# Plain fp32 instead of split halves in the inverse transforms of the first block of an H3 + MLP kernel

## The chip, the cores and the metric

The kernel runs on one core of one Trainium2 chip. The time is device microseconds of one execution. Before the change three runs took 2944.61, 2939.34 and 2942.58 us, median 2942.58. One more execution was taken by the hardware profiler: it took 2937.48 us, and the span from its first to its last instruction is 2935.7 us. Engines are named as in the profile: PE (TensorE matmul), PEld (its weight loads), DVE (VectorE), ACT (ScalarE), POOL (GpSimd), SP (SyncE, which here issues every DMA).

## The reference

Two layers A (a gated long convolution) and B (a two-layer MLP with squared ReLU) are applied in turn, twice, with a layer norm ahead of each. All is fp32, S = 2048 tokens, D = 1024 channels, F = 3584.

```python
def _A_ref(q, k, v, shift_k, ssm_k, ssm_D):
    ...
    kv = k_shift * v                      # k_shift: causal conv of k, 4 taps
    L = 2 * S
    kv_f = rfft(kv padded to L);  kf_f = rfft(ssm_k padded to L)
    y = irfft(kv_f * kf_f)[:S]
    y = y + kv * ssm_D
    return q * y

def _B_ref(x, w1, b1, w2, b2):
    h = jnp.einsum("bsd,df->bsf", x, w1) + b1
    r = jnp.where(h > zero, h, zero)
    return jnp.einsum("bsf,fd->bsd", r * r, w2) + b2

x = A_q
x = x + _A_ref(_layernorm(x), A_k, A_v, A_shift_k, A_ssm_k, A_ssm_D)
x = x + _B_ref(_layernorm(x), B_w1, B_b1, B_w2, B_b2)
x = x + _A_ref(...)          # the same two layers again
x = x + _B_ref(...)
```

The convolution in A does not depend on x, so the kernel computes it once per token block and uses it in both layers.

## The kernel before

Tokens go in four blocks of 512, channels in eight groups of 128. The convolution of a block is computed through short transforms written as matmuls with 128x128 tables of cosines and sines: forward transforms of kv (`x_part`) and of the kernel `ssm_k` (`g_part`), products of the spectra, sums, and inverse transforms. To keep fp32 accuracy on TensorE, an operand is split into a high half (a copy into the type `F32R`, made by ACT) and a low half (the rest, a subtraction by DVE or POOL), and `mm3` (L269 to L272) multiplies hi by hi, hi by lo and lo by hi into the same PSUM bank.

The work falls into two parts. `first_block` (L816) computes the convolution of block 0 for all channels, the first layer's A for it, and the first matmuls of B; in the profile it fills about the first 206 us. After that a fixed loop over matmul steps runs the MLPs of all (layer, block) pairs, while the convolutions of blocks 1 to 3 (`fwd_x`, `fwd_g`, `prod_stream`) are fed in between, step by step. The order of instructions in that loop does not depend on what `first_block` does.

In `first_block` every operation is a task of a planner (`Plan`, L86 to L169): it has a list of engines that may run it with an assumed cost for each, the keys that it reads and writes, and the ring buffers that it uses. `run` goes through the tasks greedily by assumed start times, and so fixes which engine runs a task (V is DVE, A is ACT, G is POOL, D is a DMA issue on SP) and the order on each engine. A change of tasks or assumed costs therefore reorders the whole block. A ring with n buffers makes a task wait, in the plan and on the chip, for the users of the buffer n places back.

For each channel group c the block runs `x_part`, `g_part` and then `prods(c, jj)` (L1001) for the two halves jj = 0, 1 of the block: 16 calls of `prods` in all. One call does, in this order: three products of spectra (L1009 for jj = 0; L1013 and the addition L1015 for jj = 1) into `sm` (ring of 2), two combinations (L1019, L1020), the butterfly (L538, L539) that gives z[0] and z[1], 128x256 each, and then the part that the change touches:

- L1021 takes the buffers `yl` and `yh`, rings of one buffer each;
- L1027, ACT copies z[h] into its half of `yh`, for h = 0 and 1;
- L1028, DVE or POOL subtracts: `yl` = z[h] - `yh`, for h = 0 and 1;
- L1031 calls `inverse` on the slice of 128 columns that belongs to jj: four `mm3`, 12 matmuls of 128 columns, into a bank of the ring `pt` (two banks), with the split tables `ih`, `il`, `fh`, `fl`;
- L1037 (DVE, twice) multiplies the result with the normalized x, L1040 (ACT) copies it out for `YD`, L1045 (POOL or DVE, twice) adds it to `x1`.

`inverse` (L545) is also called by `prod_stream` (L487) for blocks 1 to 3, there on all 256 columns. After the last `prods` of a half, `tail` (L1048) normalizes `x1`, transposes it (L1061) and splits it for the first matmuls of B (`weight`, L1072). The loads at the start of the block are issued at L1098 to L1100: the first kernel rows, k and v, and the table `praw`.

Of the kernel before, what the change touches and what calls it, by code (L numbers as in the profile page):

```python
# [10 lines left out]
F32 = mybir.dt.float32  # L11
F32R = mybir.dt.float32r
# [7 lines left out]
P = 128  # L20
# [7 lines left out]
BL = 256  # L28
# [143 lines left out]
def v_cost(n):  # L172
    return 130 + 1.04 * n


def g_cost(n):
    return 130 + 2.25 * n


def a_cost(n):  # L180
    return 170 + 0.84 * n
# [3 lines left out]
def tile_h3_mlp(ctx: ExitStack, tc: tile.TileContext, q, kT, vT, shk, ssmT, ssmD, w1, b1, w2, b2,  # L185
                fwd_t, pro_t, inv_t, sgn_t, out):
    nc = tc.nc
    V, A, G, PE, SY = nc.vector, nc.scalar, nc.gpsimd, nc.tensor, nc.sync
    ENG = {"V": V, "G": G}
# [3 lines left out]
    cv = ctx.enter_context(tc.tile_pool(name="cv", bufs=1))  # L193
# [75 lines left out]
    def mm3(o, lh, ll, rh, rl, start, stop):  # L269
        PE.matmul(o, lh, rh, start=start, stop=False)  # L270
        PE.matmul(o, lh, rl, start=False, stop=False)  # L271
        PE.matmul(o, ll, rh, start=False, stop=stop)  # L272
# [263 lines left out]
    def butterfly(E, s):  # L536
        y = s[:, 1:3].rearrange("p r (j u c) -> p u (r j) c", u=2, c=CG)
        E.tensor_add(flat(s, 0), y[:, 0], y[:, 1])  # L538
        E.tensor_sub(y[:, 0], y[:, 0], y[:, 1])  # L539
        return [t.rearrange("p (r n) c -> p r n c", r=2) for t in (flat(s, 0), y[:, 0])]  # L540
# [1 line left out]
    def own(t, e, g):  # L542
        return t[:, e].rearrange("p r (j g c) -> p r j g c", j=BT, g=2)[:, :, :, g % 2]

    def inverse(o, yh, yl, n=slice(0, BL)):  # L545
        tabs = ((ih[:, 1], il[:, 1], ih[:, 0], il[:, 0]), (fh[:, 3], fl[:, 3], fh[:, 2], fl[:, 2]))
        w = n.stop - n.start
        for e, (sh, sl, ch, cl) in enumerate(tabs):
            oe = o[:, e * w:e * w + w]
            mm3(oe, sh, sl, yh[:, e, 0, n], yl[:, e, 0, n], True, False)  # L550
            mm3(oe, ch, cl, yh[:, e, 1, n], yl[:, e, 1, n], False, True)

    def stats(x, mv):
        st = pre.tile([P, 2, 6], F32, name="st", bufs=2)
# [261 lines left out]
    def first_block():  # L816
        b = ORDER[0][1]
        pl = Plan()

        def new(pool, tag, n, shape, dt=F32):  # L820
            return pl.buf(tag, n, lambda: pool.tile(shape, dt, name=tag, bufs=n))
# [3 lines left out]
        def sub(tag, n, off, shape, dt=F32):  # L825
            size = math.prod(shape[1:])
            i = len(pl.rings.get(tag, ())) % n

            def make():
                v = big[dt].t[:, off + i * size:off + i * size + size]  # L830
                return v if len(shape) == 2 else v.rearrange("p (a b) -> p a b", a=shape[1])
            return pl.buf(tag, n, make, big[dt])

        def bank(tag, n, fn):
            return pl.buf(tag, n, fn)

        def dma(dst, src, r=(), w=(), cost=740, key=None):
            pl.add([("D", cost)], lambda e: SY.dma_start(dst(), src()), r, w, lat=2000)

        with tc.tile_pool(name="pro", bufs=1) as pro:  # L840
# [19 lines left out]
            def kv_load(c):  # L860
                k4 = sub("k4", 3, 0, [P, T + 3])
                v4 = new(cv, "fx", 4, [P, T])
                dma(lambda: k4.t, lambda: kT[c * P:(c + 1) * P, 0:T + 3], w=[k4])
                dma(lambda: v4.t, lambda: vT[c * P:(c + 1) * P, 0:T], w=[v4])
                return k4, v4
# [135 lines left out]
            def prods(c, jj):  # L1001
                sm = new(cv, "sm", 2, [P, 3, 2, CU])
                xs, gs = spec["x", c], spec["g", c]
                n = BL * (jj + 1)
                for ty, (xi, gi) in enumerate(PAIRS):
                    xt, gt = xs[xi], gs[gi]
                    opts = [("G", g_cost(n)), ("V", v_cost(n) + VX)]
                    if jj == 0:
                        pl.add(opts, lambda e, ty=ty, xt=xt, gt=gt: ENG[e].tensor_mul(  # L1009
                            sm.t[:, ty], xt.t[:, :, 0], gt.t[:, :, 0]), [xt, gt], [(sm, ty)])  # L1010
                        continue
                    pr = new(pro, "ppr", 3, [P, 2, BT, CU])
                    pl.add(opts, lambda e, xt=xt, gt=gt, pr=pr: ENG[e].tensor_mul(  # L1013
                        pr.t, xt.t, gt.t[:, :, ::-1]), [xt, gt], [pr])
                    pl.add([("V", v_cost(BL)), ("G", g_cost(BL) + 300)], lambda e, ty=ty, pr=pr: ENG[e].tensor_add(  # L1015
                        sm.t[:, ty], pr.t[:, :, 0], pr.t[:, :, 1]), [pr], [(sm, ty)])
                two = [("G", g_cost(BL)), ("V", v_cost(BL) + VX)]
                fl_ = lambda: sm.t.rearrange("p k g c -> p k (g c)")
                pl.add(two, lambda e: ENG[e].tensor_add(fl_()[:, 1], fl_()[:, 0], fl_()[:, 1]), [(sm, 0)], [(sm, 1)])  # L1019
                pl.add(two, lambda e: ENG[e].tensor_sub(fl_()[:, 2], fl_()[:, 0], fl_()[:, 2]), [(sm, 0)], [(sm, 2)])  # L1020
                yl, yh = new(cv, "yl", 1, [P, 2, 2, BL], F32R), new(cv, "yh", 1, [P, 2, 2, BL], F32R)  # L1021
                z = {}
                mine = lambda t, h: t[:, h, :, jj * P:jj * P + P].rearrange("p r (g c) -> p r g c", g=2)
                pl.add([("V", 2 * v_cost(BL) + VX), ("G", 2 * g_cost(BL))], lambda e: z.update(
                    enumerate(butterfly(ENG[e], fl_()))), [], [(sm, 0), (sm, 1), (sm, 2)])
                for h in range(2):
                    pl.add([("A", a_cost(BL))], lambda e, h=h: A.copy(mine(yh.t, h), z[h]), [(sm, h)], [(yh, h)])  # L1027
                    pl.add([("V", v_cost(BL)), ("G", g_cost(BL))], lambda e, h=h: ENG[e].tensor_sub(  # L1028
                        mine(yl.t, h), z[h], mine(yh.t, h).bitcast(F32)), [(sm, h), (yh, h)], [(yl, h)])
                o = bank("pt", 2, pst)  # L1030
                pl.add([("PE", 820)], lambda e: inverse(o.t, yh.t, yl.t, slice(jj * P, jj * P + P)), [(yh, 0), (yh, 1), (yl, 0), (yl, 1)], [o])  # L1031
                yo = new(cv, "fx", 4, [P, BL]) if c == KT - 1 else sub("praw", 1, 2840, [P, BL])
                yn = new(cv, "fk", 2, [P, 2, P])
                sl = slice(c * P, (c + 1) * P)
                for e_ in range(2):
                    tt = 2 * jj + e_
                    pl.add([("V", v_cost(P))], lambda e, e_=e_, tt=tt: V.scalar_tensor_tensor(  # L1037
                        yn.t[:, e_], o.t[:, e_ * P:e_ * P + P], 1.0 / BL, ns[tt].t[:, sl],
                        op0=OP.mult, op1=OP.mult), [o, (ns[tt], c // 4)], [(yn, e_)])
                pl.add([("A", a_cost(256))], lambda e: A.activation(  # L1040
                    yo.t, o.t[:, 0:BL], AF.Copy, scale=1.0 / BL), [o], [yo])
                dma(lambda: YD[0][:, 2 * jj:2 * jj + 2, sl], lambda: yo.t.rearrange("p (e c) -> p e c", e=2), [yo], cost=400)
                for e_ in range(2):
                    tt = 2 * jj + e_
                    pl.add([("G", g_cost(P)), ("V", v_cost(P) + VX)], lambda e, e_=e_, tt=tt: ENG[e].tensor_add(  # L1045
                        x1[tt].t[:, sl], x1[tt].t[:, sl], yn.t[:, e_]), [(yn, e_)], [(x1[tt], c)])
# [51 lines left out]
            gl = g_load(0)  # L1098
            kv = kv_load(0)
            dma(lambda: praw.t, lambda: pro_t, w=[praw], cost=1460)  # L1100
            pl.add([("A", a_cost(1024))], lambda e: A.copy(ptab.t[:, 0:8], praw.t), [praw], [ptab])
            pl.add([("V", v_cost(1024))], lambda e: V.tensor_sub(
                ptab.t[:, 8:16], praw.t, ptab.t[:, 0:8].bitcast(F32)), [praw], [ptab])
            for c in range(KT):
                x_part(c, *kv)
                g_part(c, *gl)
                if c + 1 < KT:
                    gl = g_load(c + 1)
                    kv = kv_load(c + 1)
                if c == 0:  # L1110
                    for t in range(NT):
                        ln_part(t)
                for jj in range(BT):
                    prods(c, jj)
                    if c == KT - 1:
                        tail(2 * jj)
                        tail(2 * jj + 1)
# [4 lines left out]
        n = 2 * AHEAD_0  # L1122
# [5 lines left out]
        return [x.t for x in xT]  # L1128

    xT = first_block()  # L1130
    pds = prod_stream()
    ml = ctx.enter_context(tc.tile_pool(name="ml", bufs=1, reuse_waits="tile"))
# [151 lines left out]
    for sb in range(1, NB):  # L1284
        if WIN[sb] > lo_u:
# [3 lines left out]
            n = sum(last_step[u] + 1 - start_step[u] - 19 * (1 - PREP_PACE) for u in range(lo_u, hi_u))  # L1289
# [16 lines left out]
    for s, (k, u, c, a, i, tts, w) in enumerate(steps):  # L1306
# [17 lines left out]
        if k == "m1":  # L1324
# [19 lines left out]
            o = rs[c, a]["o"]  # L1344
            for kk in range(4):
                t = slice(kk * P, (kk + 1) * P)
# [5 lines left out]
        else:  # L1352
            if i == 0:
                os = {tt: ps2() for tt in tts}
            r = rs[c, i]
            for tt in tts:
                t = slice(tt * P, (tt + 1) * P)
# [21 lines left out]
        if u + 1 < NU and not direct[u]:  # L1379
            n = s - start_step[u]  # L1380
# [80 lines left out]
```

## Time and profile before

| stretch of the span (us) | what runs | PE busy | DVE busy | ACT busy | POOL busy | granted PE clock |
|---|---|---|---|---|---|---|
| 0 to 206 | first block | 153.15 | 160.48 | 67.12 | 111.51 | 0.78 |
| 206 to 500 | matmul loop, convolutions beside it | 256.39 | 208.52 | 117.49 | 131.47 | 0.93 |
| 500 to 1000 | the same | 464.86 | 376.04 | 182.28 | 215.43 | 0.97 |
| 1000 to 2000 | the same | 990.24 | 682.94 | 345.67 | 425.53 | 1.00 |
| 2000 to 2935 | matmul loop | 929.47 | 279.69 | 265.69 | 33.31 | 1.00 |

The profiled execution took 2937.48 us with a span of 2935.7 us; the median of the three runs is 2942.58 us. The table is read by stretch: from 1000 us on PE is busy nearly all the time at full clock, while in the first block no engine is. "Granted PE clock" is the share of the full TensorE clock that the throttle let through, averaged over the stretch. Matmuls are pipelined in the records, each is shown until its modelled end, so the distance from one start to the next (here called the pitch) tells what a matmul costs in a row of them, and not its duration.

### The profile page before, as it was taken

The page shows a single profiled execution, that of the slowest core. Times are in us where ns is not written, and L with a number is a line of the kernel's source. Part 1 is how long each engine was busy: PE and PEld are TensorE (multiplying, and loading weights), DVE is VectorE, ACT ScalarE, POOL GpSimd, SP SyncE. Part 2 cuts the span into 40 slices and gives each one's busy share as a digit, 9 for nine tenths or more (in the row PEclk, how much of TensorE's full clock was granted, in tenths as well). Part 3 has the DMA queues.
Part 4 walks back from the last instruction along what each step waited for, and adds up shares of the span by engine and source line. Part 5 has one row for each costly group of instructions (what it writes and reads, how often), then busy time and mean ns, then how long its engine had stood idle before and what let it go on. Part 6 is the DMA issues. An engine that isn't in the chain of part 4 may idle for free.

```text
span 2935.7 us, 36250 instructions
## 1 busy us (share of the span) xinstructions
PE 2794.1 (95%) x13104; PEld 2328.6 (79%) x13104; DVE 1707.7 (58%) x2583; ACT 978.2 (33%) x1721; POOL 917.3 (31%) x649
## 2 busy tenths in 40 slices
PE   6878889879999999999999999999999999999999
PEld 6776767668888888878888888888888888888887
DVE  7867677776877777787875774353223522252122
ACT  3234434424233423444222422343223422242222
POOL 5634365433644264433655275201000100001000
PEclk8779999989999999999999999999999999999999
DMA  6357898777988889878887778565545755475543
GB/s 205 124 177 247 290 339 282 245 284 245 335 292 298 311 287 329 271 270 322 301 311 255 282 281 316 171 222 212 203 162 175 252 197 171 159 262 162 182 143 127
DMA packets 321572, 711.76 MB, mean 242 GB/s; under 512 B 31208, under 2 KB 123504, under 8 KB 321392
## 3 DMA queue, kind: packets, MB, share of 16 engines
q1 hardware_dynamic: 321392, 709.44, 70.3%
q8 instruction: 103, 1.69, 0.2%
q14 instruction: 77, 0.63, 0.1%
HBM read 578.24 MB, written 131.07 MB: 242 GB/s over the span
## 4 chain that ended last, share of the span: by engine, by line
PE 77%; DVE 10%; DMA 7%; issue 2%; POOL 2%; ACT 1%; SPq 1%; DVEq 0%; POOLq 0%; ACTq 0%
PE p L271 24%; PE p L270 24%; PE p L272 24%; DMA cg<-gd 3%; DVE whl L778 1%; PE pt L271 1%; PE pt L272 1%; POOL cp L443 1%; PE pt L270 1%; DMA xd<-fx 1%; DVE sm L447 1%; DMA wd_m<-whl 1%; PE p L649 1%; DMA whl<-wd_m 1%; DVE fx L300 1%
## 5 line engine op out<-in xcount | busy, mean ns | idle before, releaser
L443 POOL TENSOR_TENSOR cp<-cx,cg 128x384 f32<-128x384 f32 (+5 forms) x288 | 527.7, 1848 | 749.3 <-DMA cg<-gd 587.4
L271 PE MATMUL p<-whl,rh 128*128 128x512 f32 x1792 | 713.4, 398 | 15.8 <-DVE whl L778 14.1
L270 PE MATMUL p<-whl,rh 128*128 128x512 f32 x1792 | 716.0, 400 | 2.0 <-DMA whl<-wd_m 1.9
L270 PE MATMUL p<-xh,whl 128*128 128x512 f32 (+1 forms) x1840 | 708.7, 385 | 6.0 <-ACT wr L1141 4.0
L272 PE MATMUL p<-xh,whl 128*128 128x512 f32 (+1 forms) x1840 | 706.7, 384 | 5.8 <-DVE whl L778 5.8
L272 PE MATMUL p<-whl,rl 128*128 128x512 f32 x1792 | 711.9, 397 | 0.0
L271 PE MATMUL p<-xl,whl 128*128 128x512 f32 (+1 forms) x1840 | 706.5, 384 | 0.0
L1149 DVE TENSOR_TENSOR rl<-wr,rh 128x512 fp32r<-128x512 f32 x224 | 196.5, 877 | 545.0 <-ACT rh L1144 544.8
L778 DVE TENSOR_TENSOR whl<-wr,whl 128x512 fp32r<-128x512 f32 x403 | 360.9, 900 | 171.1 <-ACT whl L770 169.5
L271 PEld LDWEIGHTS p<-whl,rh 128*128 128x128 f32 x1792 | 341.2, 190 | 96.3 <-DVE whl L778 17.7
L770 ACT CAST whl<-wr 128x512 fp32r<-128x512 f32 x410 | 251.7, 618 | 469.5 <-PE p L272 363.5
L272 PEld LDWEIGHTS p<-xh,whl 128*128 128x128 f32 x1840 | 348.5, 189 | 74.5 <-DVE whl L778 6.2
L270 PEld LDWEIGHTS p<-xh,whl 128*128 128x128 f32 x1840 | 349.3, 190 | 72.8 <-ACT wr L1141 4.2
L270 PEld LDWEIGHTS p<-whl,rh 128*128 128x128 f32 x1792 | 341.1, 190 | 80.1 <-DMA whl<-wd_m 2.3
L272 PEld LDWEIGHTS p<-whl,rl 128*128 128x128 f32 x1792 | 340.7, 190 | 80.0
L271 PEld LDWEIGHTS p<-xl,whl 128*128 128x128 f32 x1840 | 349.0, 190 | 65.8 <-DVE xl L1068 0.3
L1141 ACT ACTIVATE wr<-p,b1t 128x512 f32<-128x512 f32 x222 | 153.2, 690 | 699.4 <-PE p L272 693.2
L1269 POOL TENSOR_TENSOR acc<-acc,px 128x1024 f32<-128x1024 f32 x32 | 86.2, 2726 | 788.4 <-DMA px<-b 773.3
L1155 DVE TENSOR_TENSOR acc<-p,acc 128x512 f32<-128x512 f32 x248 | 166.8, 688 | 250.2 <-PE p L272 249.4
L447 DVE TENSOR_REDUCE sm<-cp 128x128 f32<-128x384 f32 (+5 forms) x288 | 249.8, 875 | 92.8 <-POOL cp L443 92.8
L1142 ACT ACTIVATE wr<-wr 128x512 f32<-128x512 f32 x224 | 141.8, 633 | 7.1
L1144 ACT CAST rh<-wr 128x512 fp32r<-128x512 f32 x224 | 139.2, 621 | 7.1
(200 smaller groups left out, 2556.6 us busy)
## 6 DMA issues: line engine op xcount, KB each, us to landing
whl<-wd_m SPq DMA_DIRECT2D x500, 512.0 KB, 4.3
wr<-w SPq DMA_DIRECT2D x418, 256.0 KB, 4.7
wd_m<-whl SPq DMA_DIRECT2D x70, 512.0 KB, 6.1
cx<-xd SPq DMA_DIRECT2D x48, 512.0 KB, 5.9
cg<-gd SPq DMA_DIRECT2D x48, 512.0 KB, 5.9
gd<-fg SPq DMA_DIRECT2D x72, 256.0 KB, 6.7
cx<-xd SPq DMA_DIRECT2D x48, 384.0 KB, 5.2
cg<-gd SPq DMA_DIRECT2D x48, 384.0 KB, 6.5
```

What stands on the lines that cost most here:

```text
L270: PE.matmul(o, lh, rh, start=start, stop=False)
L271: PE.matmul(o, lh, rl, start=False, stop=False)
L272: PE.matmul(o, ll, rh, start=False, stop=stop)
L443: G.tensor_mul(pr.rearrange("p c i -> p i c"), xt[:, 0:j + 1], gt[:, j::-1])
L447: V.tensor_reduce(sm[:, ty, jj], st["pr"], axis=AX.X, op=OP.add)
L770: A.copy(t[:, 0], raws[n]["t"])
L778: ENG[e[n % len(e)]].tensor_sub(t[:, 1], raws[n]["t"], t[:, 0].bitcast(F32))
L1141: A.activation(r, st["o"], AF.Relu, bias=b1t[:, st["f"]:st["f"] + 1])
L1142: A.activation(r, r, AF.Square)
L1144: A.copy(st["hi"], r)
L1149: V.tensor_sub(st["lo"], st["r"]["t"], st["hi"].bitcast(F32))
L1155: V.tensor_add(accs[tt][:, d], o, accs[tt][:, d])
```

## The change

Only `prods` in `first_block`, the loads at its start, and the now unused argument of `inverse` change. The butterfly's results z[0] and z[1] go to TensorE as they are, in plain fp32, and are multiplied by plain fp32 tables: two matmuls accumulate into each half of the bank, four in all. The copies L1027, the subtractions L1028 and the use of `yl` and `yh` as halves are gone from the first block. The buffer named `yh` holds the four tables in `first_block` instead (`itab`, 128x4x128), filled by four DMAs of 64 KB each, issued after `praw` and ahead of the second channel group's loads. The assumed cost of the inverse in the plan goes from 820 to 1300.

```diff
-    def inverse(o, yh, yl, n=slice(0, BL)):
+    def inverse(o, yh, yl):
         tabs = ((ih[:, 1], il[:, 1], ih[:, 0], il[:, 0]), (fh[:, 3], fl[:, 3], fh[:, 2], fl[:, 2]))
-        w = n.stop - n.start
         for e, (sh, sl, ch, cl) in enumerate(tabs):
-            oe = o[:, e * w:e * w + w]
-            mm3(oe, sh, sl, yh[:, e, 0, n], yl[:, e, 0, n], True, False)
-            mm3(oe, ch, cl, yh[:, e, 1, n], yl[:, e, 1, n], False, True)
+            oe = o[:, e * BL:e * BL + BL]
+            mm3(oe, sh, sl, yh[:, e, 0], yl[:, e, 0], True, False)
+            mm3(oe, ch, cl, yh[:, e, 1], yl[:, e, 1], False, True)
...
-                yl, yh = new(cv, "yl", 1, [P, 2, 2, BL], F32R), new(cv, "yh", 1, [P, 2, 2, BL], F32R)
                 z = {}
-                mine = lambda t, h: t[:, h, :, jj * P:jj * P + P].rearrange("p r (g c) -> p r g c", g=2)
                 pl.add([("V", 2 * v_cost(BL) + VX), ("G", 2 * g_cost(BL))], lambda e: z.update(
                     enumerate(butterfly(ENG[e], fl_()))), [], [(sm, 0), (sm, 1), (sm, 2)])
-                for h in range(2):
-                    pl.add([("A", a_cost(BL))], lambda e, h=h: A.copy(mine(yh.t, h), z[h]), [(sm, h)], [(yh, h)])
-                    pl.add([("V", v_cost(BL)), ("G", g_cost(BL))], lambda e, h=h: ENG[e].tensor_sub(
-                        mine(yl.t, h), z[h], mine(yh.t, h).bitcast(F32)), [(sm, h), (yh, h)], [(yl, h)])
                 o = bank("pt", 2, pst)
-                pl.add([("PE", 820)], lambda e: inverse(o.t, yh.t, yl.t, slice(jj * P, jj * P + P)), [(yh, 0), (yh, 1), (yl, 0), (yl, 1)], [o])
+
+                def back(e):
+                    for h in range(2):
+                        oe = o.t[:, h * P:h * P + P]
+                        for r in range(2):
+                            PE.matmul(oe, itab.t[:, 2 * h + r], z[h][:, r], start=r == 0, stop=r == 1)
+                pl.add([("PE", 1300)], back, [(sm, 0), (sm, 1), *((itab, i) for i in range(4))], [o])
...
             dma(lambda: praw.t, lambda: pro_t, w=[praw], cost=1460)
+            itab = new(cv, "yh", 1, [P, 4, P])
+            for i, src in enumerate((inv_t[:, 1], inv_t[:, 0], fwd_t[:, 3], fwd_t[:, 2])):
+                dma(lambda i=i: itab.t[:, i], lambda src=src: src, w=[(itab, i)], cost=200)
```

## The prediction

> **What bounds the kernel now.** I read the stretches first, because one average over the span hides that the change lives in one stage.
>
> ```profile
> span 2935.7 us, 36250 instructions
> ...
> 0.00:206.00 206.00, 153.15 (x974) 146.00 (x975) 160.48 (x295) 67.12 (x137) 111.51 (x122) 0.78 0.52 167
> ...
> 2000.00:2935.00 935.00, 929.47 (x4083) 762.03 (x4081) 279.69 (x467) 265.69 (x433) 33.31 (x12) 1.00 0.54 185
> ...
> 30.00:190.00 160.00, 123.52 (x787) 117.54 (x786) 129.64 (x218) 47.82 (x104) 100.68 (x107) 0.76 0.43 138
> ```
>
> Columns: stretch, length, busy us of PE, PEld, DVE, ACT, POOL, granted clock, DMA share, GB/s. Late in the span PE is all but full and DVE idles. In the first block (0 to 206) DVE is the fullest engine, PE second at a clock of 0.78, and neither is full: this stage is bound by a chain that hops between the two. What comes after is a fixed order that starts when the block hands over, so I let what the block gains or loses pass to the end one to one. From 30 to 190 us `prods` runs; the chain of waits there, by line:
>
> ```profile
> by line: PE p L271 9.1%; issue 8.8%; PE p L270 8.3%; PE p L272 8.2%; PE pt L271 6.0%; PE pt L272 5.2%; PE pt L270 4.5%; DVE yl L1028 4.4%; DVE sm L538 4.2%; DVE ppr L1013 4.0%; DVE sm L539 2.8%; DVE sm L1019 2.7%; DVE sm L1009 2.7%; DVE sm
> ```
>
> The three "PE pt" lines are the inverses (15.7% of 160 us), "DVE yl" the subtraction that feeds them (4.4%). Counted piece by piece the chain holds 24.8 us in 137 inverse matmuls, 11.4 of the 16 inverses (137 / 12), at a mean 0.181 us, and 7.1 us of `yl` on DVE with 0.9 on POOL. One link in order of time (start, us, what):
>
> ```profile
> 178.80 0.42 DVE sm L538
> ...
> 179.25 0.42 DVE sm L539
> 179.67 0.67 DVE sm L1015 x2
> 180.34 0.87 DVE yl L1028
> 181.22 0.04 issue
> 181.26 0.48 PE pt L271
> ...
> 183.66 0.23 PE pt L272
> 183.88 0.02 issue
> 183.91 0.39 ACT fx L1040
> ```
>
> The butterfly ends at 179.67; the subtraction waits behind an addition, and the result can be read out only at 183.91.
>
> **The change, part by part.**
>
> *Removed, L1028 and L1027.* All instructions of the block:
>
> ```profile
> L1028 DVE TENSOR_TENSOR yl<-sm,yh 128x256 fp32r<-128x256 f32 x24 | 15.5, 672 | 0.2 <-ACT yh L1027 0.2
> L1027 ACT CAST yh<-sm 128x256 fp32r<-128x256 f32 x32 | 12.2, 404 | 24.8 <-DVE sm L538 21.8 <-DVE sm L539 2.7
> ```
>
> The 24 DVE subtractions are 15.5 us of the fullest engine; 8 more take 6.9 us of POOL (mean 866 ns). On the chain they are 7.1 + 0.9 = 8.0 us: that is the saving I count. The 32 copies are not on the chain, and ACT is busy 48 of 160 us: they count nothing. Were they uncovered, each would be 0.4 us.
>
> *Replaced, 12 split matmuls by 4 plain ones.* No row shows a plain fp32 matmul that is not a transpose, so its pitch has to be bounded. Starts at full clock:
>
> ```profile
> 109.42 0.28 PE L272 MATMUL pt<-yh,il 128*128 128x128 f32 x1
> 109.54 0.27 PE L270 MATMUL pt<-yh,fh 128*128 128x128 f32 x1
> ...
> 1499.96 0.39 PE L272 MATMUL p<-xh,whl 128*128 128x512 f32 x1
> 1500.19 0.39 PE L270 MATMUL p<-xh,whl 128*128 128x512 f32 x1
> ```
>
> A split matmul of 128 columns has a pitch of 0.111 us (109.20 to 110.09, eight steps), one of 512 columns 0.228 (1499.73 to 1500.64, four steps); at the low clock the former is 0.213 (181.54 to 183.46, nine steps). The chain's mean 0.181 is thus 1.63 times the full-clock pitch. From below: a plain matmul costs what a split one does, 0.111. From above: an exact product of two operands, each a high and a low half, has four partial products, of which `mm3` makes three with one matmul each; four at 0.111 are 0.444. Between: 256 columns have a pitch of 0.118 (18.17 to 19.35, ten steps) and 512 of 0.228, 0.43 ns a column, so 128 columns alone take 0.055 and four times that 0.22. I take 0.22, since it is the 512-column row, the same count of columns streamed; the 128-column pitch is clearly not set by columns. On the chain 137 / 12 x 4 = 45.7 plain matmuls stand for 137: at 0.22 x 1.63 = 0.36 they take 16.5 us, 8.3 less than 24.8. At the low end (0.181 each) 8.3 us, 16.5 less; at the high end (0.72) 33.1, 8.3 more.
>
> The Trainium skill speaks against this edit: "True FP32: 4 passes through PE array" (FP8 and Floating Point Precision, section TensorE Precision Notes), so 16 passes would replace 12; no run here shows it yet. At one split pitch a pass that would be the high end above, at column time alone the value taken.
>
> *Added, four table loads.* SP issues a DMA every 0.47 us at this place (4.88, 5.35, 5.82), so what stands behind (k and kernel rows of group 1, the q rows) goes out 4 x 0.47 = 1.9 us later. DVE has no idle time ahead of the first statistics on q (14.30), so most is covered by its own queue; uncovered it is 1.9. I take 1.
>
> *Moved, the plan.* In the order that the changed kernel is built with, DVE runs 280 instructions of the block instead of 298, POOL 111 instead of 125. Besides the subtractions, DVE takes 11 of POOL's additions L1045 (about 0.5 us each, +5.3) and gives up three L1015, three of L1019/L1020/L538, two L539 and two L881 (-2.4, -2.9, -1.3, -2.4); the other moves (two L1013 +2.4, two L921 +1.5, one each of L1009 and L987 +1.3, one L590 -0.1) bring its sum to -14.1 us, POOL's likewise to about -10. On PE and SP the sequence of transforms keeps its pattern. The new wait, PE for the butterfly itself, stands where PE waited for `yh` and `yl` (22.6 us of PE idle time in this stretch: 13.4 for the copy, 8.7 + 0.5 for `yl`); queued behind it are the next group's transforms, as before. `sm` is now held until PE has read it, not until the subtraction; the inverse two calls back stands in PE's order ahead of, or right behind, the x transforms that the next writer needs, so I cost that at nothing; if it showed, DVE and POOL products (L1009, L1015) would wait about one inverse, 1 to 2 us.
>
> *Sum.* By the chain: -8.3 - 8.0 + 1 = -15.3. What is late next is DVE's queue: it can give only its own -14.1, with its 30 us of idle time kept, so -14.1 + 1 = -13. I take the smaller. From the profiled execution, 2937.5 - 13 = 2924.5; it lies 5.1 under the median of the runs shown (2942.6), and against that median the forecast is 2929.6, rounded to 2930.
>
> **The rivals.**
>
> 1. *The plain matmul costs four split ones (0.444).* Then +8.3 - 8.0 + 1 = +1: 2942.6 + 1 = 2944. For it: a four-part product is what fp32 accuracy asks. Against: partial products share the same table, and columns alone need half.
>
> 2. *Slower: the plain matmul loads each half of its table without cover.* A weight load of these groups lasts 0.188 us; two and four times 0.055 are 0.60. On the chain 45.7 x 0.60 x 1.63 = 44.7, so +19.9 - 8.0 + 1 = +13: 2955. It decides from 0.43 us a matmul on (45.7 x 1.63 x 0.43 = 32, the gain is gone) and is plainly slower from 0.51. Against: in the rows shown loads run beside the matmul before.
>
> 3. *Slower: PE's clock.* PE pieces of the transforms (25.6% of 160 = 41 us) and the new inverses (16.5) stand on the chain at 0.76. At 0.62 they grow by 57.5 x (0.76 / 0.62 - 1) = 13 and eat all, at 0.55 by 22, so +9: 2952. For it: windows of 20 us show anything from 0.50 to 1.00, and PE gets shorter bursts. Against: the change shortens PE's gaps. By the Trainium skill (TensorE: Matmul & The Clock Gate, Part 1) the clock is half or full, and falls after an idle window of about 3.4 us; the 3 us gaps ahead of 40.34 and 43.86 fit, and the change would remove rather than add such gaps.
>
> 4. *The gain is hidden.* From 206 to 500 the DMA share is 0.85 and PE 256 of 294 busy; if transfers there did not move up with the hand-over, the end would stay: 2942. Against: SP issues the loop's first loads from 190.70 on, behind the block's last stores, so they move too.
>
> **How the numbers follow.** The forecast holds 0.63, rival 1 0.11, rival 4 0.07, rival 2 0.12, rival 3 0.07. About 0.2%, 5.9 us, is what a measurement of this kernel can tell from no change: the forecast gives faster, 1 and 4 the same, 2 and 3 slower. Range: at the cheapest matmul -16.5 - 8.0 = -24.5, 2918; at the dearest row-bound with all of the table loads uncovered +8.3 - 8.0 + 1.9 = +2, 2945. That leaves out rivals 2 and 3.
>
> **What would show it.** Right: the inverse's four matmuls 0.2 to 0.25 us apart at full clock; no `yl` before the loop; the first block's hand-over (last L1061 transposes, at 204 us now) near 191; the stretches after it as long as before. Wrong: a pitch over 0.43 us, a mean clock under 0.62 from 30 to 190 us, PE idle for `sm` longer than 23 us, or an earlier hand-over with the same end.

## The result: 1% faster, more than twice what was forecast

The changed kernel took 2913.45 us (median of four runs, 2909.61 to 2915.96) against 2943.57 us for the kernel before (four runs, 2939.34 to 2944.61): a ratio of 0.9899, 95% interval 0.9884 to 0.9915, so 25 to 34 us less. The forecast was 13 us less, 2930, with a range down to 2918: right in sign, under half in size, and the measured time lies below the range.

The profile after, by stretches (columns as before: busy us of PE, PEld, DVE, ACT, POOL, granted clock, DMA share, GB/s), the row from 30 us to the first transposes of `tail`:

```profile
span 2914.2 us, 36055 instructions
...
30.00:163.90 133.90, 103.61 (x715) 97.16 (x714) 114.64 (x207) 36.50 (x71) 89.73 (x94) 0.82 0.53 167
```

DVE is busy in 114.6 of 133.9 us, where it was 129.6 of 160: not only its work fell but its idle time too, from 30 to 19 us. The clock rose from 0.76 (0.75 if the stretch before runs to its first transposes, 190.7 us) to 0.82. The chain of waits from 30 to 172 us:

```profile
by line: PE p L271 10.1%; PE p L272 8.7%; PE p L270 8.3%; issue 7.5%; DVE fx L877 7.1%; DVE sm L539 4.1%; DVE sm L538 3.7%; DVE cp L986 3.0%; DVE sm L1014 2.9%; POOL sm L1008 2.7%; PE p L347 2.4%; DVE fk L1036 2.4%; PE pt L1029 2.2%; POOL s
```

The inverses, 24.8 us of the chain before, are 2.2% of these 142 us, 3.1 us. The hand-over is read from the last transposes of the first block (name, count, shortest / median / longest ns, first to last start), first in the kernel before, then in the changed one:

```profile
L1061 PE MATMUL p<-ident,px x8: 272/272/273, 204.0 to 204.8; 128*128 128x128 f32 x8
```

```profile
L1060 PE MATMUL p<-ident,px x8: 270/272/273, 177.2 to 177.9; 128*128 128x128 f32 x8
```

The block ends 26.9 us earlier. From there to the end of the span the profiled execution before took 2730.9 us and the one after 2736.3; over all profiled executions of this study that rest lies between 2730.9 and 2740.0 with no clear relation to the hand-over. The spans differ by 21.5 us because the rest before happened to be the shortest of all; the medians of the runs differ by 30. The hand-over leaves the spread of the rest out and is therefore used below beside the run times. It is read from one profiled execution of each kernel: the median time less the hand-over lies between 2734.6 and 2740.7 over all kernels of the table, so a difference of two or three us between two hand-overs is no more than this scatter.

### The profile page after: what moved, and what is told of

Same layout as the page of the kernel before. It is cut to its first block, busy times and chain, and to the rows that moved or that the text cites. A ratio compares the mean times of both kernels' runs of the same rounds, so it can differ in the third digit from the quotient of the medians.

```text
span 2914.2 us, 36055 instructions
## 1 busy us (share of the span) xinstructions
PE 2783.6 (96%) x13040; PEld 2315.0 (79%) x13040; DVE 1681.8 (58%) x2565; ACT 965.6 (33%) x1687; POOL 902.7 (31%) x635
## 4 chain that ended last, share of the span: by engine, by line
PE 75%; DVE 10%; DMA 8%; POOL 2%; issue 2%; ACT 1%; SPq 1%; DVEq 0%; POOLq 0%; ACTq 0%
PE p L271 24%; PE p L270 24%; PE p L272 24%; DMA cg<-gd 4%; POOL cp L443 2%; DMA xd<-fx 2%; DVE whl L777 1%; PE pt L271 1%; PE pt L272 1%; PE pt L270 1%; DVE sm L447 1%; DMA whl<-wd_m 1%; PE p L648 1%; DVE fx L300 1%; DVE rl L1151 1%
```

## The experiments

Three theories for the 14 us of hand-over (26.9 less 13) that the sum lacked. A: the split itself, as work for DVE and as a link (butterfly, copy, subtraction, then matmul) that PE waits for. B: the new order that the planner made. C: a warmer TensorE clock. All kernels in one table; "clock" is from 30 us to the first transposes of `tail`, "hand-over" the start of the last transposes. The ratio is to the kernel before, measured beside it.

| kernel | hand-over us | clock | median us | before us | ratio, 95% interval |
|---|---|---|---|---|---|
| before | 204.8 | 0.75 | 2943.57 | | |
| changed | 177.9 | 0.82 | 2913.45 | 2943.57 | 0.9899, 0.9884 to 0.9915 |
| split_in_order | 202.1 | 0.74 | 2938.44 | 2943.57 | 0.9986, 0.9976 to 0.9997 |
| idle_split | 188.2 | 0.79 | 2924.5 | 2943.57 | 0.9937, 0.9918 to 0.9955 |
| plain_twice | 175.4 | 0.94 | 2914.32 | 2943.57 | 0.9897, 0.9875 to 0.992 |
| two_halves | 206.5 | 0.75 | 2947.17 | 2943.57 | 1.001, 0.9995 to 1.0026 |
| cost_820 | 177.6 | 0.87 | 2913.61 | 2947.21 | 0.9891, 0.987 to 0.9913 |
| cost_2000 | 170.5 | 0.85 | 2906.5 | 2947.21 | 0.9865, 0.9846 to 0.9884 |
| before_cost_1300 | 196.9 | 0.76 | 2934.47 | 2947.21 | 0.9961, 0.9946 to 0.9976 |
| no_table_loads | 179.7 | 0.82 | 2917.4 | 2947.21 | 0.99, 0.9877 to 0.9924 |
| plain_in_old_order | 181.6 | 0.84 | 2921.44 | 2945.2 | 0.9918, 0.9897 to 0.9939 |
| before_twice | 231.0 | 0.74 | 2967.84 | 2945.2 | 1.0076, 1.0061 to 1.0091 |
| before_cost_2000 | 193.6 | 0.76 | 2930.82 | 2945.2 | 0.995, 0.9935 to 0.9965 |
| plain_twice_2000 | 171.1 | 0.93 | 2905.69 | 2945.2 | 0.9859, 0.9841 to 0.9877 |
| before_warm_4 | 202.6 | 0.85 | 2940.21 | 2942.23 | 0.9994, 0.9978 to 1.0011 |
| before_warm_8 | 211.6 | 0.87 | 2947.76 | 2942.23 | 1.0023, 1.0007 to 1.004 |
| split_kind_no_split | 180.0 | 0.83 | 2915.63 | 2942.23 | 0.992, 0.9893 to 0.9946 |

### The split put back into the new order

```diff
                 def back(e):
...
                     for h in range(2):
+                        A.copy(mine(hl2[0], h), z[h])
+                        V.tensor_sub(mine(hl2[1], h), z[h], mine(hl2[0], h).bitcast(F32))
...
-                        for r in range(2):
-                            PE.matmul(oe, itab.t[:, 2 * h + r], z[h][:, r], start=r == 0, stop=r == 1)
+                        mm3(oe, sh, sl_, hl2[0][:, h, 0], hl2[1][:, h, 0], True, False)
+                        mm3(oe, ch, cl, hl2[0][:, h, 1], hl2[1][:, h, 1], False, True)
```

> The changed kernel's plan and order, but the task of the inverse does the split work of before: two ACT copies, two DVE subtractions (all 32 on DVE) and 12 split matmuls, placed where the plain matmuls stood. If the planner's new order made the extra gain (theory B), this stays near the changed kernel: 2913 to 2923 us, hand-over (first of the last transposes of px) at 177 to 187 us. If the split itself costs the time, as work and as a link that PE waits for (theory A), the gain is gone: 2937 to 2955 us, hand-over at 200 to 215 us.

Hand-over 202.1, 24.2 us later than the changed kernel in its own order; 2938 us. Theory A's numbers. The new order without the new arithmetic is worth 2.7 us (204.8 to 202.1); that holds two things that the kernel before does not have, the table loads, which stay, and all 32 subtractions on DVE instead of 24.

### The split as idle work

The same copies and subtractions, but PE multiplies the sums as in the changed kernel; nobody reads the halves.

> The changed kernel with the split's 32 copies and 32 subtractions kept as idle work: ACT and DVE do them at the place of the inverse, nobody reads them, PE multiplies the sums in plain fp32. If the gain came from the link that PE no longer waits for (theory A1), at most a third is given back: 2913 to 2923 us. If it came from DVE's own time (15.5 us of subtractions; theory A2, as my sum had it), half or more is given back: 2927 to 2940 us.

2924.5 us falls between the two expectations, and the hand-over says why: idle work alone costs 10.3 us (177.9 to 188.2), and having PE read it, with 12 matmuls for 4, another 13.9 (188.2 to 202.1). Both halves of theory A are real. DVE's busy time shows that the link is gone here, not the work; the first row is split_in_order, the second idle_split:

```profile
30.00:188.50 158.50, 122.81 (x777) 114.88 (x777) 132.15 (x239) 47.88 (x103) 89.31 (x94) 0.74 0.45 141
30.00:175.20 145.20, 102.16 (x700) 95.24 (x700) 129.50 (x236) 48.36 (x103) 87.94 (x93) 0.79 0.48 151
```

129.5 us of DVE, as many as before (129.6), yet in a stretch of 145 us and not 160: without the link DVE idles 16 us, where it idled 30 in the kernel before and 26 in split_in_order.

### Twice the matmuls, in either kernel

```diff
-                        for r in range(2):
+                        for k in range(4):
+                            r = k % 2
                             PE.matmul(oe, itab.t[:, 2 * h + r], z[h][:, r], start=r == 0, stop=r == 1)
```

> The changed kernel with each pair of plain matmuls done twice, the same result: 8 instead of 4, some 1.8 us more per inverse at full clock than none, 0.9 more than the changed kernel. By my sum 11.4 inverses stand on the chain at 0.36 us a matmul, so 2930 us. If the inverses have left the chain (3.1 us of them are in the changed kernel's chain), 2914 to 2919 us.

And in the kernel before, `inverse` called twice per task:

> The kernel before with each inverse done twice, 24 split matmuls instead of 12, the same result. In the changed kernel twice the matmuls cost nothing, at a higher clock. If the inverses stand on the chain here (theory A), 11.4 of them at 12 x 0.11 to 0.18 us more: 2956 to 2968 us, less what a warmer clock gives back. If a warmer clock pays for them all (theory C): 2938 to 2948 us at a clock over 0.85 from 30 us to the last transposes.

The same question gets opposite answers. In the kernel before, 12 more split matmuls per inverse move the hand-over by 26.2 us, 1.64 us for each of all 16 inverses (12 at 0.136). In the changed kernel four more plain ones move it by -2.5, nothing. The stretches, kernel before with twice the matmuls, then the changed kernel with twice:

```profile
30.00:216.80 186.80, 152.37 (x976) 146.27 (x975) 128.47 (x219) 47.96 (x104) 101.11 (x107) 0.74 0.37 118
```

```profile
30.00:162.20 132.20, 105.98 (x835) 101.88 (x834) 116.13 (x204) 36.23 (x71) 88.42 (x93) 0.94 0.53 168
```

In the first, PE's added 29 us (152.4 against 123.5) lengthen the stretch nearly in full: an inverse there sits between two waits. In the second the clock went from 0.82 to 0.94, so the other matmuls got shorter: PE is busy only 2.4 us longer (106.0 against 103.6). This run alone does not say what the added matmuls would cost at an unchanged clock. In its chain the inverses are back with 23.8 us, and the hand-over is no later for it.

### One pair of halves for the whole block

Each half of the block gets its own key in one pair of tiles, so that calls for jj = 0 and 1 need not take turns.

> The kernel before with one pair of split tiles for the whole block and a key for each half of it, so that the calls for jj = 0 and 1 no longer take turns on a ring of one; the plan orders anew. If that ring made the inverses stand on the chain (theory A3), 2925 to 2937 us; if not, 2939 to 2947 us, the spread of a new order.

206.5, no gain. The plan ordered anew as well, and the next runs show what orders alone move, so this says that freeing the ring did not bring the gain, not that the ring costs nothing.

### Other orders of each kernel

Only the assumed cost of the inverse changes: 820 and 2000 in the changed kernel, 1300 and 2000 in the kernel before.

> The changed kernel with the plan's assumed cost of the inverse back at 820: only the order changes. If the extra gain is luck of one order (theory B), the time moves by 8 us or more from 2913, to 2922 or above. If the split's removal makes it, 2908 to 2919 us.

> The changed kernel with the assumed cost at 2000: a third order. Theory B: 2922 us or above; theory A: 2908 to 2919 us.

> The kernel before with the assumed cost of the inverse at 1300, all its work kept: only the order changes. Theory B (an order is worth 10 us or more): 2933 us or less, or 2953 or more. Theory A: 2938 to 2949 us.

> The kernel before with the assumed cost of the inverse at 2000, all its work kept. With 820 and 1300 this gives three orders of each kernel. If orders spread by some 8 us in both and the change is worth 19 to 27 us in each (theory A with a spread): 2930 to 2945 us. If the better orders go with the higher cost, as with the changed kernel at 2000: 2925 to 2932 us.

An order is worth more than theory A allowed: 7.9 and 11.2 us in the kernel before (204.8 to 196.9 and 193.6), 7.4 in the changed one (177.9 to 170.5). At the same assumed cost the change is worth 27.2 (820), 19.0 (1300) and 23.1 us (2000), so no single order explains it. At 2906.5 us cost_2000 also beats both kernels; with the matmuls doubled, below, it is no better.

### The new arithmetic in the old order

The kernel before with its plan untouched: the tasks of the split issue nothing, PE's task does the changed kernel's matmuls, the table loads follow `praw`.

> The kernel before with its own plan and order, every task in its place, but the copies and subtractions issue nothing and the inverse is the changed kernel's four plain matmuls with its table loads: the change without the new order. Theory A (the split, as work and as the link that PE waits for, makes the gain): 2912 to 2924 us, hand-over at 176 to 188 us, PE's inverses under 8 us of the chain. Theory B (the new order made what my sum lacked): 2926 to 2936 us, hand-over near 192 us.

```profile
30.00:167.20 137.20, 105.21 (x735) 99.62 (x734) 114.50 (x199) 38.25 (x75) 96.49 (x101) 0.84 0.51 163
```

Hand-over 181.6, 23.2 us of the 26.9 with no task moved, and DVE's work is that of the changed kernel (114.5 against 114.6). The remaining 3.7 go with the new order; by the run times it would be some 6 (2921 here is 24 under its kernel before, the changed kernel 30 under its own), with four runs between 2914.8 and 2929.1. The inverses are 8.5 us of its chain, just over the 8 expected.

### Without the table loads

> The changed kernel without the four table loads: the high halves of the tables, already in SBUF, stand in for the full tables (the low halves of the tables are left out of the product). My sum gave the loads 1 us, 0 to 1.9: 2911 to 2914 us, and the first block shorter by as much. If the loads hold up the start, 2908 us or less.

2917.4 us, and the hand-over came 1.8 us later, not earlier; taking the four tasks out also made another order. The loads' cost is below what orders scatter by and stays open within that.

### The clock

The kernels so far with split inverses have a clock of 0.74 to 0.76 in the stretch, those with plain ones 0.79 to 0.94. To see whether that made the gain, plain matmuls of a constant were put ahead of the inverse in the kernel before, meant for the time in which PE waits anyway:

```diff
+                def back(e):
+                    for i in range(4):
+                        PE.matmul(o.t[:, 0:P], ident, ident, start=True, stop=True)
+                    inverse(o.t, yh.t, yl.t, slice(jj * P, jj * P + P))
...
```

> The kernel before, all its work and order kept, with four plain fp32 matmuls of constants ahead of each inverse, into the bank that the inverse then overwrites; PE does them where it waits for the split halves. If the clock makes the part of the gain that my sum lacked (theory C): clock at 0.82 or more from 30 us to the last transposes, hand-over at 190 to 199 us, 2928 to 2938 us. If only the split's link does (theory A): hand-over at 204 us or later, 2943 to 2960 us.

> The same with eight, 1.8 us of PE at full clock ahead of each inverse. Theory C: clock over 0.85, hand-over under 200 us, 2925 to 2939 us. Theory A: no gain, 2945 to 2970 us, since 16 x 1.8 us can't all lie in waits.

```profile
30.00:188.70 158.70, 128.14 (x925) 123.29 (x923) 130.54 (x222) 49.06 (x107) 103.75 (x108) 0.85 0.44 141
```

With four the clock is 0.85, above the changed kernel's 0.82, and the hand-over only 2.2 us earlier; the time is the same as before. With eight it is 0.87 and 6.8 us later. Theory C's hand-over (190 to 199) did not come, and theory A's (204 or later) was missed by 1.4 us. The test does not price the clock by itself, since the added matmuls did not all fall into waits. Its chain of waits from 30 to 188.7 us (L1034 is the added matmuls):

```profile
by line: issue 8.9%; PE p L271 8.7%; PE p L272 7.9%; PE p L270 7.8%; PE pt L1034 5.8%; DVE sm L538 5.1%; PE pt L271 4.7%; DVE yl L1028 4.5%; DVE ppr L1013 4.0%; DVE sm L539 3.9%; PE pt L272 3.9%; DVE sm L1015 3.7%; DVE fx L878 3.4%; PE pt L
```

5.8% of 158.7 us are 9.2 us of added matmuls on the chain, which can hide a gain of the clock of about that size. An estimate from the chain before: its 41 us of transforms and 24.8 of inverses would be some 5 us shorter at 0.82 than at 0.76. The opposite cut is the changed kernel with one plain matmul of each sum kept, so that PE waits for the same, and 12 split matmuls of constant halves in place of the other two (it leaves part of the inverse out):

> The changed kernel with the inverse as one plain matmul of each sum (so PE waits for the same as there) and 12 split matmuls of constant halves: PE's work of before without the split and its link (the inverse is left out of the result but for a part). PE's time at full clock, 12 x 0.11 + 2 x 0.23 = 1.8 us, is that of the kernel with the plain matmuls done twice, which handed over at 175 us at a clock of 0.94. Theory C (the kind of matmul keeps the clock up): clock at 0.80 or less, hand-over at 185 us or later, 2921 to 2935 us. If only the split's link counts (theory A): hand-over at 174 to 182 us, 2909 to 2918 us.

```profile
30.00:165.70 135.70, 114.68 (x828) 110.77 (x827) 114.14 (x204) 36.20 (x71) 87.51 (x93) 0.83 0.51 162
```

180.0: without the split, the kind and number of PE's matmuls are worth 2.1 us of the 26.9. PE does 11 us more than in the changed kernel (114.7 against 103.6) at the same clock (0.83 against 0.82), and the block hardly notices. Its chain from 30 to 165.7 us runs along PE nonetheless:

```profile
by line: PE p L271 16.4%; PE p L272 15.2%; PE p L270 14.7%; PE pt L1029 7.0%; PE pt L272 5.4%; PE pt L271 5.3%; PE pt L270 4.0%; issue 3.3%; DVE ppr L1012 2.4%; PE p L347 2.3%; DVE fk L1038 2.2%; DVE cp L986 2.1%; DVE fg L886 2.0%; POOL fx 
```

The four "PE pt" lines are 21.7%, 29 us, more than the 24.8 of the kernel before, at a hand-over 24.8 us earlier. So theory A carries the larger part: with the split and its link gone, 12 split matmuls and two plain ones are nearly as good as four plain ones. What the warmer clock adds by itself is not separated: every kernel whose PE does not wait for the split has one (0.79 to 0.94).

### Doubled matmuls at a cost of 2000

> The changed kernel at an assumed cost of 2000 and with each pair of plain matmuls done twice. If a warmer clock pays for the added matmuls in any order (theory C), 2900 to 2908 us at a clock over 0.90; if it was that one order, 2909 to 2918 us.

2905.7 us at 0.93, hand-over 171.1 against 170.5 without doubling: the added matmuls cost nothing at the warmer clock in this order too, and gain nothing.

## Why the prediction was half right, step by step

**What bounds the kernel.** Right: the block is a chain between engines that are not full, and what it gains reaches the end one to one within the spread of the rest (2730.9 to 2740.0). The hand-over, forecast near 191, came at 177.9.

**The price of a plain matmul.** Right. It is recorded as two weight loads and two matmuls; a piece of the changed kernel's chain (start, us, what):

```profile
92.13 0.94 PE pt L1029 x8
```

Eight records are four plain matmuls, 0.235 us each among transforms at 0.12; taken was 0.22. The two ends, 0.111 and 0.444, were both off. The Trainium skill's "True FP32: 4 passes through PE array" (FP8 and Floating Point Precision, TensorE Precision Notes) agrees with the trace if a pass costs the columns' time, four times 0.055, and not a split matmul's pitch. Rivals 1 and 2, which hung on a dearer matmul, fall with this.

**The inverses on the chain, with DVE's queue as the cap. This is the step that failed.** The prediction said that 45.7 plain matmuls "stand for 137" on the chain and left 16.5 us of them there; then it cut the gain to what DVE's own work gives. Measured on the chain: 3.1 us. With this 13.4 us less, the sum's -15.3 would have been -28.7, against the -26.9 of the block. But such a share says where the time stood and not what it was worth: plain_twice and split_kind_no_split have 23.8 and 29 us of inverses on their chains and hand over 29.4 and 24.8 us ahead of the kernel before. What the step is worth is priced by putting the split back: 10.3 us for its work, 13.9 for PE having to wait for it and read it with 12 matmuls, and 2.7 for the new order. The inverses cost time because of what they wait for more than because of their length. With the split in place, matmuls added behind it cost nearly their full time (before_twice, +26.2); with it away, 14 mixed ones for four cost 2.1 us at the same clock, and eight plain ones nothing at a warmer one.

**DVE as what is late next.** The cap of -14.1 "with its 30 us of idle time kept" set the forecast of -13, and it was wrong for the same reason. Its work fell by 15 us (129.6 to 114.6), near the 14.1 of the sum; the idle time fell by 11, since much of it was waiting at the far end of the link (idle_split, with the work kept, idles 16). In the new order the 8.0 us taken for the split on the chain stand against 10.3 for the work alone (idle_split) and 13.9 for the link with the longer PE part.

**Table loads, at 1 us**: not contradicted, not resolved. **The plan at nothing beyond its moves**: off by some 3 to 4 us of hand-over in this change, and by up to 11 between orders of the kernel before, which the prediction had no term for.

**PE's wait for the butterfly.** Right that it takes the place of the old one. PE's idle time ahead of the inverses, in the changed kernel (who waits for whom, us in total, times, longest):

```profile
PE pt L1029 <- POOL sm L538: 11.7, 4, 4.6
PE pt L1029 <- DVE sm L538: 7.6, 3, 6.6
PE pt L1029 <- POOL sm L539: 0.7, 3, 0.2
```

20.0 us, hardly under the 22.6 of before. PE waits nearly as long in all; its wait now ends with the butterfly, and the subtraction that came between is gone.

**The clock rival.** Its sign was wrong: the clock rose, though hardly for the reason given against it, since 20.0 us of gaps ahead of the inverses stayed, up to 6.6 us long (the rows above). The forecast itself had kept the clock at its value of before. Rival 4, a hidden gain, did not happen.

**The range** was built from the bounds of the matmul's price alone. The larger unknown, whether the inverses stay on the chain at all, had no end in it; with none of them there and no cap it would have reached 2942.6 - 24.8 - 8.0 = 2910.

## What to carry to other kernels

When a step that sits between two waits is removed, price the whole link that it closes (here copy, subtraction and the matmuls behind them), with "nothing of it stays on the chain" as one end of the range; its share of the chain, and the next engine's busy time with today's idle time added, are not limits. Ask of each piece on a chain whether it is there for its length or for what it waits for: doubling it, in both versions, tells the two apart, if the clock stays as it was; here it did not, and a run with nearly as much added work at the same clock had to decide. Where a planner sets the order, time a few orders of each version before a gain of some microseconds is put down to the change.

## What the runs showed of the hardware that was not expected

The granted TensorE clock did not follow PE's busy share alone. 192 more split matmuls of 128 columns left it at 0.74 with PE busy in 82% of the stretch (before_twice, 152.4 of 186.8 us); 64 more plain ones brought it from 0.82 to 0.94 at 80% (plain_twice, 106.0 of 132.2), and 64 in the kernel before from 0.75 to 0.85 at 81% (before_warm_4). The kind of matmul is not the whole of it either: with 192 split matmuls that wait for no halves, and 32 plain ones, it was 0.83 at 85% (split_kind_no_split). A split matmul of 128 columns has a pitch of 0.111 us for about 0.055 us of columns, a plain one 0.235 for 0.22, so the clock may follow the share of time in which columns stream; that was not tried by itself.
